# Row maxima of the masked scores: the unread output goes to the scores' own PSUM bank instead of SBUF

## The chip, the cores and the metric

One Trainium2 chip, of which the program uses one core. The metric is the device time of one execution in microseconds (us). Times of engines, tiles and waits come from a hardware profile of one execution. The engines are PE (matrix products), PEld (PE's weight loads), DVE (VectorE), ACT (ScalarE), POOL (GpSimd) and SP (which issues DMAs). PSUM is the memory that PE writes to, in banks of 512 fp32 per partition; SBUF is the other on-chip memory.

## What is computed

A transformer block on 2048 tokens of width 576: a modulated layer norm, causal attention in four segments of 512 tokens with 32 heads of width 18 and a running memory, a second layer norm, and a feed-forward part of width 4608. What matters here is the softmax inside a segment:

```python
for s in range(N):                                   # 4 segments of L = 512
    qs, ks, vs = q[:, :, s], k[:, :, s], v[:, :, s]
    logits = jnp.einsum("bhqd,bhkd->bhqk", qs, ks) * scale + mask
    p = _softmax(logits, axis=-1)
    a_dot = jnp.einsum("bhqk,bhkd->bhqd", p, vs)
    ...
    o = g * a_mem + (1.0 - g) * a_dot
```

The softmax needs the maximum of each row of masked scores.

## The kernel before

The work is cut into 32 units: four segments times eight groups of four heads. Each unit goes through two passes.

**Pass 1 (`p1_step`, lines 208 to 233)** finds the row maxima. For each of the four blocks of 128 query rows, from the last (`i = 3`, 512 keys) to the first (`i = 0`, 128 keys), PE computes scores of each head into a PSUM bank (L218; the tile is called `s` in the profile, tag `s1`, three banks in turn). DVE then makes one pass over each head's scores (L223): it adds the causal mask `tri`, takes the maximum along the row, and puts that into a column of `mx`. The instruction shows as two rows, the pass itself (CUSTOM_DVE_ANT_0) and the reading of its accumulator (DVE_READ_ACCUMULATOR2_ANT, tile `mx`). It also has to write the masked scores somewhere, and nobody reads them. With 512 and 384 keys a bank holds one head, with 256 keys two heads and with 128 keys four, so a unit has 16 DVE passes on 11 banks: four banks of 512, four of 384, two of 256 and one of 128.

After a unit's last pass POOL negates and splits the maxima (L229 to L232, tile `mc`), PE transposes them (L238, tile `pmt`), ACT copies them out (L242, `mr`) and two DMAs write them as extra rows under the unit's queries. **Pass 2 (`p2_step`)** multiplies keys by these extended queries (L715), so that the scores come out with the maximum subtracted; ACT takes the exponential (L722, tile `Pt`), POOL clears what the mask hides (L726) and PE multiplies by the values (L739, `av`).

Where the work stands:

- Units 0 and 1 do pass 1 in the first stage, beside the projections (L113). There `jp` is None, and the unread output is always the same 512 bf16 of a scratch tile (`xw`).
- Units 2 to 31 do pass 1 in the attention stage, one unit for each turn of the loop over `u` (L1509), two units ahead of pass 2. A turn has 11 steps `k`. Each step issues a bit of pass 2, then one bank of pass 1, and then the events of the table `PAT`: output projection of earlier segments (L857), memory terms (L925), weights of the output projection (L1020 to L1022), stores, and so on. So the 256-key and 128-key banks stand in steps 8 to 10, at the end of a turn. The order is written out by hand; each engine works through its own list in that order.
- In that stage the unread output goes to tiles called `junk`, bf16, four buffers in turn (`jb` is 4).

A DVE instruction that writes where an earlier DVE instruction wrote waits for that one on DVE's own semaphore. With one scratch tile the earlier one is the pass just before; with four buffers it is four passes back.

Of the kernel before, what the change touches and what calls it, by code (L numbers as in the profile page):

```python
# [9 lines left out]
BF16 = mybir.dt.bfloat16  # L10
# [5 lines left out]
P = 128  # L16
# [6 lines left out]
L = 512  # L23
# [55 lines left out]
def f32(ap):  # L79
    return ap.bitcast(F32)  # L80
# [3 lines left out]
def block(ctx: ExitStack, tc: tile.TileContext, x, wqk, wv, wo, beta, wgu, wgr, wd, c, crow, w_mod, w_mod0, w_mod1, w_modc, xt, out):  # L84
    nc = tc.nc
    def pool(stk, name, bufs=1, **kw):
        return stk.enter_context(tc.tile_pool(name=name, bufs=bufs, reuse_waits="tile", **kw))
# [42 lines left out]
    xw = pool(ctx, "xw").tile([P, 2304], F32, tag="xw", name="xw")  # L130
# [27 lines left out]
    tri = vst.tile([P, L], F32, tag="tri", name="tri")  # L158
# [49 lines left out]
    def p1_step(u, b, i, ps, jp, jb):  # L208
        if i == 3:
            mcol[u] = (mwk.tile([P, 4, 4], F32, tag="mx", name="mx"),  # L210
                       mwk.tile([P, 2, 4, 4], F32R, tag="mc", name="mc"))
        mx, mc = mcol[u]
        n = 128 * (i + 1)
        per = L // n if n <= 256 else 1
        for h0 in range(0, 4, per):
            bank = ps.tile([P, L], F32, tag="s1", name="s1", bufs=SB[-1])
            for h in range(h0, h0 + per):
                nc.tensor.matmul(bank[:, n * (h - h0):n * (h - h0) + n],  # L218
                                 lhsT=qst[b][0:108, h, 128 * i:128 * i + 128],
                                 rhs=kst[b][0:108, h // 2, 0:n], start=True, stop=True)  # L220
            for h in range(h0, h0 + per):
                junk = jp.tile([P, L], BF16, tag="junk", name="junk", bufs=jb) if jp else xw[:, 2000:2256].bitcast(BF16)
                nc.vector.tensor_tensor_reduce(junk[:, :n], bank[:, n * (h - h0):n * (h - h0) + n], tri[:, L - n:],  # L223
                                               1.0, -3e38, op0=ALU.add, op1=ALU.max, accum_out=mx[:, h, i:i + 1])
            if h0 + per < 4:
                yield
        if i == 0:
            eng = nc.gpsimd
            eng.tensor_scalar(mc[:, 0], mx, -1.0, 0.0, op0=ALU.mult, op1=ALU.add)  # L229
            lo = mwk.tile([P, 4, 4], F32, tag="ml", name="ml")  # L230
            eng.tensor_tensor(lo, mx, f32(mc[:, 0]), op=ALU.add)
            eng.tensor_scalar(mc[:, 1], lo, -1.0, 0.0, op0=ALU.mult, op1=ALU.add)  # L232
        yield
# [11 lines left out]
    def p1_unit(u, b, ps, tag, bufs, jp, jb):  # L245
        for i in range(4):
            yield from p1_step(u, b, 3 - i, ps, jp, jb)
        for i in range(3):
            yield
        mt_a(u, ps, tag, bufs)  # L250
        mt_b(u)
# [30 lines left out]
    with ExitStack() as p1:  # L282
# [74 lines left out]
        with ExitStack() as p0:  # L357
# [36 lines left out]
            for b in range(3):  # L394
                n = P if b < 2 else 64
# [303 lines left out]
    def p1_seq(u):  # L699
        if NE <= u < NU:  # L700
            for i in range(4):
                yield from p1_step(u, u % NB, 3 - i, ps, wk, 4)
# [798 lines left out]
    with tc.manual_schedule():  # L1501
# [69 lines left out]
        for i in range(4):  # L1571
            for h in range(2):
                for c in range(WC):
                    n = 8 * i + 4 * h + c
# [32 lines left out]
        n, nw = 0, PF  # L1607
# [216 lines left out]
```

## Time and profile before

| | |
|---|---|
| median of 3 runs | 1817.38 us (1816.68 to 1819.77) |
| the profiled execution: its time | 1818.94 us |
| its span, first to last instruction | 1816.9 us |
| PE busy | 1789.4 us (98% of the span) |
| DVE busy | 1484.1 us (82%) |
| ACT busy | 1086.4 us (60%) |
| POOL busy | 675.3 us (37%) |
| DVE passes of L223 with junk output | 480, of 484 ns on average |
| first and last of them | at 229.5 us and 550.2 us of the span |

The profiled execution took 1.56 us more than the median. Its busy times say how long instructions of an engine were under way; a matmul's end is modelled, so a busy PE is not always PE at full rate. The attention stage is the stretch from about 230 to 560 us; what comes behind it (up to 1816.9 us) is the feed-forward part, which has no instruction of the change.

### The profile page before, as it was taken

The page shows a single profiled execution, that of the slowest core. Times are in us where ns is not written, and L with a number is a line of the kernel's source. Part 1 is how long each engine was busy: PE and PEld are TensorE (multiplying, and loading weights), DVE is VectorE, ACT ScalarE, POOL GpSimd, SP SyncE. Part 2 cuts the span into 40 slices and gives each one's busy share as a digit, 9 for nine tenths or more (in the row PEclk, how much of TensorE's full clock was granted, in tenths as well). Part 3 has the DMA queues.
Part 4 walks back from the last instruction along what each step waited for, and adds up shares of the span by engine and source line. Part 5 has one row for each costly group of instructions (what it writes and reads, how often), then busy time and mean ns, then how long its engine had stood idle before and what let it go on. Part 6 is the DMA issues. An engine that isn't in the chain of part 4 may idle for free.

```text
span 1816.9 us, 31453 instructions
## 1 busy us (share of the span) xinstructions
PE 1789.4 (98%) x10627; PEld 1521.8 (84%) x10627; DVE 1484.1 (82%) x3365; ACT 1086.4 (60%) x2374; POOL 675.3 (37%) x1110
## 2 busy tenths in 40 slices
PE   7999999999999999999999999999999999999999
PEld 5888866777777888888888888888888888888888
DVE  7556388888886899889889889858888888888886
ACT  4334288878776567777777777534544544544542
POOL 3444078775467656656656656200000000000000
PEclk9999999999999999999999999999999999999999
DMA  8768766667657655455455454594334324324331
GB/s 270 258 225 281 265 209 195 195 203 227 168 167 239 209 181 171 144 175 176 142 177 174 122 168 145 168 311 148 98 105 126 98 92 130 106 80 130 107 103 53
DMA packets 146116, 306.26 MB, mean 169 GB/s; under 512 B 30917, under 2 KB 61765, under 8 KB 144165
## 3 DMA queue, kind: packets, MB, share of 16 engines
q1 hardware_dynamic: 134772, 260.19, 46.8%
q10 hardware_dynamic: 11184, 44.07, 6.2%
q8 instruction: 85, 1.39, 0.3%
q14 instruction: 75, 0.61, 0.1%
HBM read 198.69 MB, written 104.94 MB: 167 GB/s over the span
## 4 chain that ended last, share of the span: by engine, by line
PE 91%; DMA 3%; DVE 2%; ACT 1%; issue 1%; POOL 1%; SPq 0%; ACTq 0%; DVEq 0%; POOLq 0%
PE A L1343 25%; PE pd L1462 20%; PE C L1343 13%; PE B L1343 6%; PE pp L113 5%; PE s L218 4%; PE av L739 3%; PE pv L113 3%; PE s L715 3%; PE pw L857 3%; PE pd L1482 3%; DVE junk L223 1%; PE pn L925 1%; PE pm L550 1%; PE px L760 1%
## 5 line engine op out<-in xcount | busy, mean ns | idle before, releaser
L1343 PE MATMUL A<-y,wh 128*128 128x512 f32 x1152 | 404.1, 391 | 0.7 <-ACT cu L1372 0.7
L1470 DVE TENSOR_TENSOR acc<-acc,pd 128x576 f32<-128x576 f32 x327 | 245.0, 750 | 78.3 <-PE pd L1462 71.9
L1462 PE MATMUL pd<-dh,ah 128*128 128x288 f32 x896 | 267.4, 298 | 0.0
L1462 PE MATMUL pd<-dl,ah 128*128 128x288 f32 x896 | 263.7, 294 | 0.0
L1462 PE MATMUL pd<-dh,al 128*128 128x288 f32 x896 | 262.4, 293 | 0.0
L223 DVE CUSTOM_DVE_ANT_0 junk<-s,tri 128x512 bf16<-128x512 f32 (+1 forms) x480 | 207.2, 484 | 56.0 <-PE s L218 41.4
L1343 PEld LDWEIGHTS A<-y,wh 128*128 128x128 f32 x1152 | 216.2, 188 | 39.2 <-ACT cu L1372 1.1
L1304 DVE TENSOR_TENSOR wl<-O,wh 128x256 fp32r<-128x256 f32 x504 | 240.2, 480 | 1.6 <-ACT wh L1303 0.9
L1343 PE MATMUL A<-y,wl 128*128 128x512 f32 x576 | 224.5, 390 | 0.0
L722 ACT ACTIVATE Pt<-s 128x512 f32<-128x512 f32 (+1 forms) x352 | 182.6, 558 | 45.3 <-PE s L715 29.2
L1343 PE MATMUL C<-y,wh 128*128 128x512 f32 x576 | 202.7, 393 | 0.0
L1303 ACT CAST wh<-O 128x256 fp32r<-128x256 f32 x504 | 198.3, 406 | 2.0 <-POOL O L1297 1.7
L1462 PEld LDWEIGHTS pd<-dh,ah 128*128 128x128 f32 x896 | 168.1, 188 | 18.5 <-ACT pd L1438 3.9
L1462 PEld LDWEIGHTS pd<-dl,ah 128*128 128x128 f32 x896 | 169.5, 189 | 16.2
L1408 DVE TENSOR_TENSOR al<-sg,ah 128x512 fp32r<-128x512 f32 x240 | 177.2, 739 | 6.8 <-ACT ah L1407 6.5
L1297 POOL TENSOR_TENSOR O<-O 128x128 f32<-128x128 f32 x280 | 155.6, 589 | 71.1 <-DMA O<-in_wgu_dram 37.6
L1462 PEld LDWEIGHTS pd<-dh,al 128*128 128x128 f32 x896 | 169.1, 189 | 0.0
L1407 ACT CAST ah<-sg 128x512 fp32r<-128x512 f32 x240 | 149.0, 621 | 25.8 <-DVE sg L1367 24.9
L1343 PEld LDWEIGHTS C<-y,wh 128*128 128x128 f32 x576 | 108.0, 188 | 18.8
L1343 PEld LDWEIGHTS A<-y,wl 128*128 128x128 f32 x576 | 108.2, 188 | 14.9
L1343 PE MATMUL A<-y,wr 128*128 128x512 f32 x288 | 113.6, 394 | 0.0
L1343 PE MATMUL C<-y,wl 128*128 128x512 f32 x288 | 112.1, 389 | 0.0
(400 smaller groups left out, 4141.8 us busy)
## 6 DMA issues: line engine op xcount, KB each, us to landing
wr<-rD SPq DMA_DIRECT2D x216, 112.0 KB
O<-in_wgu_dram SPq DMA_DIRECT2D x36, 512.0 KB
oD<-O ACTq DMA_DIRECT2D x36, 512.0 KB
O<-oD SPq DMA_DIRECT2D x36, 512.0 KB
O<-in_wgu_dram SPq DMA_DIRECT2D x36, 384.0 KB
y<-yD SPq DMA_DIRECT2D x11, 1024.0 KB
ks<-kD SPq DMA_DIRECT2D x72, 144.0 KB
kD<-fh SPq DMA_DIRECT2D x16, 512.0 KB
```

Of the source, the lines that this page charges most:

```text
L113: nc.tensor.matmul(ps, lhsT=a, rhs=b, start=(k == 0), stop=(k == 13))
L218: nc.tensor.matmul(bank[:, n * (h - h0):n * (h - h0) + n], lhsT=qst[b][0:108, h, 128 * i:128 * i + 128], rhs=kst[b][0:108, h // 2, 0:n], s ...
L223: nc.vector.tensor_tensor_reduce(junk[:, :n], bank[:, n * (h - h0):n * (h - h0) + n], tri[:, L - n:], 1.0, -3e38, op0=ALU.add, op1=ALU.max ...
L722: nc.scalar.activation(pt[:, h:h + per, :n], bank[:, :n * per].rearrange("p (a b) -> p a b", a=per), AF.Exp, scale=SCALE)
L1297: eng.tensor_tensor(o[:, d, i, s_], o[:, a, i, s_], o[:, b, i, s_], op=op)
L1303: nc.scalar.copy(wh, o)
L1304: later.append(lambda: nc.vector.tensor_tensor(wl, o, f32(wh), op=ALU.subtract))
L1343: nc.tensor.matmul(bank, lhsT=a, rhs=b, start=(first and n == 0), stop=(n == 6), skip_group_check=not first)
L1407: nc.scalar.copy(ah, src)
L1408: later.append(lambda: nc.vector.tensor_tensor(al, src, f32(ah), op=ALU.subtract))
L1462: nc.tensor.matmul(pd[:, i, :288], lhsT=a[:, tk], rhs=w, start=(add and k == 0), stop=(k == 2), skip_group_check=not add)
L1470: nc.vector.tensor_tensor(o, o, pd[:, :, :288], op=ALU.add)
```

## The change

The row-maximum instruction writes the masked scores over the scores that it reads, in fp32, in the same part of the same PSUM bank. The tiles `junk` and the scratch output in `xw` are no longer written. The mask, the maximum and everything that reads `mx` stay.

```diff
             for h in range(h0, h0 + per):
-                junk = jp.tile([P, L], BF16, tag="junk", name="junk", bufs=jb) if jp else xw[:, 2000:2256].bitcast(BF16)
-                nc.vector.tensor_tensor_reduce(junk[:, :n], bank[:, n * (h - h0):n * (h - h0) + n], tri[:, L - n:],
+                nc.vector.tensor_tensor_reduce(bank[:, n * (h - h0):n * (h - h0) + n], bank[:, n * (h - h0):n * (h - h0) + n], tri[:, L - n:],
                                                1.0, -3e38, op0=ALU.add, op1=ALU.max, accum_out=mx[:, h, i:i + 1])
```

The order of the instructions on each engine stays the same in the attention stage; what differs is which instruction waits for which. These are rows of DVE's list at the end of a unit in that stage, before the change: the second pass of a bank of 256 keys, and the first and second of the bank of 128 keys (`_2766` and `_2790` are bank numbers; the names in brackets are the engines whose semaphores an instruction waits for).

```order
L773 TENSOR_TENSOR o_2512<-px,r_2758 128x4x72 [waits DMAHW4_49,DMAHW3_49,DMAHW7_49,DVE_49,Activation_49]
L223 ISA junk,mx<-s_2766,tri 128x256 [waits PE_49]
L223 ISA mx 128x1
L223 ISA junk,mx<-s_2766,tri 128x256
...
L223 ISA junk,mx<-s_2790,tri 128x128 [waits DVE_49,PE_49]
...
L223 ISA junk,mx<-s_2790,tri 128x128 [waits DVE_49]
```

The second 256-key pass waits for nothing, and the 128-key passes wait for the pass four places back that wrote the same buffer. The same place with the change (its lines are numbered one lower):

```order
L772 TENSOR_TENSOR o_2512<-px,r_2734 128x4x72 [waits DMAHW4_49,DMAHW3_49,DMAHW7_49,DVE_49,Activation_49]
L222 ISA s_2742,mx<-s_2742,tri 128x256 [waits PE_49]
L222 ISA mx 128x1
L222 ISA s_2742,mx<-s_2742,tri 128x256 [waits DVE_49]
...
L222 ISA s_2762,mx<-s_2762,tri 128x128 [waits PE_49]
...
L222 ISA s_2762,mx<-s_2762,tri 128x128 [waits DVE_49]
```

Two passes on one bank now both write that bank, so the later one waits for the one directly in front of it: in a unit the second pass of each 256-key bank and the last three passes of the 128-key bank. In the first stage it is the other way round: there every pass waited for the one before it (one scratch tile), and now only passes on a shared bank do. There the scheduler also moves a few instructions by one or two places.

## The prediction

> **What bounds the kernel now.** I start with the page: busy times and the chain that ended last.
>
> ```profile
> PE 1789.4 (98%) x10627; PEld 1521.8 (84%) x10627; DVE 1484.1 (82%) x3365; ACT 1086.4 (60%) x2374; POOL 675.3 (37%) x1110
> PE 91%; DMA 3%; DVE 2%; ACT 1%; issue 1%; POOL 1%; SPq 0%; ACTq 0%; DVEq 0%; POOLq 0%
> ```
>
> PE carries the end. The change touches DVE only, and only in the stretches where L223 stands, so next come the busy times by window for the attention stage (columns: length, then PE, PEld, DVE, ACT, POOL busy with instruction counts) and, for the same stage, the chain's shares by line.
>
> ```profile
> 230.00:330.00 100.00, 95.28 (x722) 66.35 (x721) 83.83 (x368) 86.02 (x192) 77.78 (x137) 1.00 0.66 200
> 330.00:430.00 100.00, 98.88 (x787) 77.32 (x787) 82.04 (x354) 79.02 (x172) 68.76 (x129) 1.00 0.66 202
> 430.00:530.00 100.00, 98.82 (x791) 76.60 (x790) 85.72 (x362) 76.72 (x164) 54.86 (x106) 1.00 0.67 190
> by line: PE s L218 18.4%; PE av L739 17.7%; PE s L715 15.8%; PE pw L857 10.4%; DVE junk L223 5.7%; PE pn L925 3.9%; PE px L760 3.3%; ACT Pt L722 3.2%; DMA xr<-in_x_dram 3.1%; issue 3.0%; DMA woraw<-in_wo_dram 1.7%; PE pv L113 1.2%; DMA rD<-
> ```
>
> PE is busy 95 to 99% there and DVE 82 to 86%. The passes of L223 are nevertheless 5.7% of the chain over these 335 us, 19 us: DVE is close behind PE, and sometimes ahead of it in the chain. Who waits for whom (total us, times, longest):
>
> ```profile
> DVE junk L223 <- PE s L218: 41.4, 26, 14.8
> PEld s L218 <- DVE mx L223: 10.7, 37, 1.0
> L223 DVE CUSTOM_DVE_ANT_0 junk<-s,tri 128x512 bf16<-128x512 f32 x120 | 77.1, 681 | 53.7 <-PE s L218 39.7 <-POOL mc L232 4.9 <-POOL yh L1161 4.3
> ```
>
> PE's weight loads wait for DVE 37 times, DVE waits for PE longer. The last row says where: the idle time of DVE lies ahead of 512-key passes, that is at the start of a unit. Without the very first wait (14.8 us) it is 38.9 us over 29 starts, **1.34 us a unit**. That gap is the cover for whatever DVE gains or loses at the end of a unit.
>
> **Part one: passes that wait for the pass in front of them.** The attention stage shows passes without such a wait, the first stage (one scratch tile) passes with it. First without, for 256 and 128 keys (columns: start, duration):
>
> ```profile
> 263.07 0.42 DVE L223 CUSTOM_DVE_ANT_0 junk<-s,tri 128x256 bf16<-128x256 f32 x1
> 263.42 0.42 DVE L223 CUSTOM_DVE_ANT_0 junk<-s,tri 128x256 bf16<-128x256 f32 x1
> ...
> 264.32 0.28 DVE L223 CUSTOM_DVE_ANT_0 junk<-s,tri 128x128 bf16<-128x128 f32 x1
> 264.53 0.29 DVE L223 CUSTOM_DVE_ANT_0 junk<-s,tri 128x128 bf16<-128x128 f32 x1
> ```
>
> And with it:
>
> ```profile
> 94.30 0.41 DVE L223 CUSTOM_DVE_ANT_0 xw<-s,tri 128x256 bf16<-128x256 f32 x1
> 94.76 0.42 DVE L223 CUSTOM_DVE_ANT_0 xw<-s,tri 128x256 bf16<-128x256 f32 x1
> ...
> 99.35 0.29 DVE L223 CUSTOM_DVE_ANT_0 xw<-s,tri 128x128 bf16<-128x128 f32 x1
> 99.68 0.29 DVE L223 CUSTOM_DVE_ANT_0 xw<-s,tri 128x128 bf16<-128x128 f32 x1
> ```
>
> Start to start is 0.35 against 0.46 us with 256 keys and 0.21 against 0.33 us with 128: the wait costs 0.11 and 0.12 us, though the durations stay. A unit gets two of the first and three of the second, 2 x 0.11 + 3 x 0.12 = **0.58 us**, and 30 units 17.4 us of DVE time. If nothing hid it the kernel would be 1% slower.
>
> [...]
>
> Most of the 0.58 us is hidden by the gap of 1.34 us. It shows where that cover is thin. These rows are starts of units (in brackets the idle time before); at 287.21 the instruction before it ends at 287.07:
>
> ```profile
> 247.70 0.69 DVE L223 CUSTOM_DVE_ANT_0 junk<-s,tri 128x512 bf16<-128x512 f32 x1 [0.37 <-PE s L218]
> 257.50 0.69 DVE L223 CUSTOM_DVE_ANT_0 junk<-s,tri 128x512 bf16<-128x512 f32 x1 [0.59 <-PE s L218]
> 286.31 0.76 DVE L1022 TENSOR_TENSOR wol<-woraw,woh 128x576 fp32r<-128x576 f32 x1 [0.39 <-ACT woh L1020]
> 287.21 0.69 DVE L223 CUSTOM_DVE_ANT_0 junk<-s,tri 128x512 bf16<-128x512 f32 x1
> 540.23 0.69 DVE L223 CUSTOM_DVE_ANT_0 junk<-s,tri 128x512 bf16<-128x512 f32 x1 [0.63 <-PE s L218]
> ```
>
> The shortfall is 0.58 - 0.37 = 0.21 at the first and 0.58 - 0.14 = 0.44 at the third, **0.65 us** together; the other two just suffice. A second way is the maxima's own path: DVE, then POOL, then PE's transpose, which stands in PE's list with everything queued behind it. Its thinnest place is the last but one unit:
>
> ```profile
> 540.28 0.20 POOL L232 TENSOR_SCALAR mc<-ml 128x16 fp32r<-128x16 f32 x1
> 540.54 0.28 PE L238 MATMUL pmt<-ident,mc 128*32 128x128 f32 x1
> ```
>
> POOL ends at 540.48, PE starts at 540.54: of 0.58 us, **0.52** reach PE. A third is the one stretch in which the chain itself runs through the end of a unit, to L1022 and the DMA whose buffer that frees (pieces of the chain: start, length):
>
> ```profile
> 262.82 0.33 DVE junk L223
> ...
> 265.04 0.68 DVE wol L1022
> 265.73 5.60 DMA woraw<-in_wo_dram
> ```
>
> All **0.58** count there. In the first stage the change takes waits away, two semaphores at a time with 512 keys, as these rows (with the wait, and without) show:
>
> ```profile
> 88.30 0.69 DVE L223 CUSTOM_DVE_ANT_0 xw<-s,tri 128x512 bf16<-128x512 f32 x1
> 89.15 0.69 DVE L223 CUSTOM_DVE_ANT_0 xw<-s,tri 128x512 bf16<-128x512 f32 x1
> ...
> 258.12 0.69 DVE L223 CUSTOM_DVE_ANT_0 junk<-s,tri 128x512 bf16<-128x512 f32 x1
> 258.73 0.69 DVE L223 CUSTOM_DVE_ANT_0 junk<-s,tri 128x512 bf16<-128x512 f32 x1
> ```
>
> That is 0.85 against 0.61, but the chain of that stage is projections on PE and meets such a pair once: **-0.24 us**. The instructions that move by a place or two there are covered by the projections; should one be late, its cost is of the same size. Sum of part one: 0.65 + 0.52 + 0.58 - 0.24 = **+1.5 us**.
>
> **Part two: a pass that writes PSUM.** No DVE instruction of before writes PSUM, so I bound it.
>
> ```profile
> L1389 ACT COPY B<-A 128x512 f32<-128x512 f32 x71 | 40.3, 568 | 45.3 <-PE A L1343 44.4
> L1372 ACT COPY tc<-A 128x512 f32<-128x512 f32 x72 | 42.2, 586 | 107.3 <-PE A L1343 107.2
> L1408 DVE TENSOR_TENSOR al<-sg,ah 128x512 fp32r<-128x512 f32 x240 | 177.2, 739 | 6.8 <-ACT ah L1407 6.5
> L469 DVE TENSOR_TENSOR hl<-x,hh 128x512 fp32r<-128x512 f32 x12 | 7.8, 686 | 13.6 <-ACT hh L468 13.6
> 68.46 1.89 DVE L469 TENSOR_TENSOR hl<-x,hh 128x512 fp32r<-128x512 f32 x3 [3.59 <-ACT hh L468]
> ```
>
> On ACT the same copy takes 568 ns into PSUM (L1389) and 586 into SBUF: -18 ns, the lower end. The most that two DVE rows of one size differ by where their data lie and who else is at work is 739 against 686: +53 ns, the upper end. The nearest row is DVE's own: three passes of L469, all in SBUF, take 1.89 us, so 0.60 from start to start, while L223, which reads PSUM, has 0.61. PSUM costs DVE 0.01 us as a source; I take **+10 ns** for it as a destination too. The chain has 19 us of such passes; their mean pitch is (0.61 + 0.48 + 0.35 + 0.21) / 4 = 0.41 (the 384-key pitch lies between its neighbours), so 46 of them: 46 x 0.01 = **+0.5 us**. The gap of 1.34 us hides the rest (16 x 0.01 = 0.16 us a unit).
>
> [...]
>
> **The sum.** 1.5 + 0.5 = +2.0 us. On the profiled execution's 1818.94 that makes 1820.9; it ran 1.56 us above the median, so in medians **1819.4 us** (+0.11%). What a measurement can tell from no change is about 0.2%, 3.6 us: below 1813.7 is faster, above 1821.0 slower.
>
> **The rivals.**
>
> *Slower: the PSUM write lengthens every pass.* At the upper end of 53 ns a unit has 16 x 0.053 = 0.85 us more, with the waits 1.43 against a gap of 1.34. DVE then sets the pace at most unit starts: 0.09 x 29 = 2.6 us if all gaps were alike; as they go from 0.14 up, I reckon twice that, 5. With 46 x 0.053 = 2.4 on the chain and 1.5 of part one that is +9: **1826.4**. It decides from about 20 ns on: 46 x 0.02 = 0.9, and the four thin starts above lose 0.3 each, 1.2, which with 1.5 makes 3.6. For it: PE waits for DVE 37 times. Against it: the ACT rows and the 10 ns. Chance 0.31.
>
> *Slower: POOL passes the delay on.* The 512-key row blames 4.9 us of unit starts on POOL mc L232, five times by the waits. If that is real, the gap there does not cover: mc itself comes later by 0.58, five times 2.9 us: +4.9, **1822.3**. Against it: these passes wait for PE too, and the last semaphore named need not be the one that held. Chance 0.10.
>
> *Slower by much: read and write take turns in the bank.* Pitches give (0.61 - 0.21) / 384 = 1.04 ns a column, 5120 columns a unit, 5.3 us more; less the gap 4 us, 30 times: near 1937. Nothing speaks for it but that no row excludes it. Chance 0.03, outside the range.
>
> *No change: the waits cost nothing.* If DVE would have stood still between two passes on one bank anyway, part one vanishes with its early gain, 0.5 us stays, **1817.8**. Against it stand the paired rows. Chance 0.04. [...]
>
> *Faster: the write to PSUM is cheap.* At ACT's -18 ns the unit loses only 0.58 - 0.29 = 0.29 us: 0.15 + 0.23 + 0.29 - 0.24 - 46 x 0.018 = -0.4, **1817.0**, still no change (0.07). To be faster by 0.2% each pass would have to lose some 80 ns, the whole fixed part of a 128-key pass (0.21 - 128 x 0.00104 = 0.08): -46 x 0.08 = -3.7. Chance 0.06, **1813.5**.
>
> **Chances and range.** Forecast 0.39, no cost 0.04, ACT's price 0.07: within 0.2% 0.50. Slower 0.31 + 0.10 + 0.03 = 0.44, faster 0.06. The range goes from 1815.8 (ACT's price and a little more) to 1828.0 (53 ns and some more shortfall).
>
> **What the profile after would show.** Part one: 256-key passes on one bank 0.46 apart, 128-key passes 0.33, and gaps at unit starts smaller by about 0.6 us; PE's waits for DVE hardly more than 10.7 us. Part two: passes of 512 keys 0.61 to 0.62 apart. Wrong if that pitch is 0.63 or more, or if waits of PE for DVE grow by several us (DVE sets the pace), or if pairs on one bank still stand 0.35 apart (no cost).

## The result, and the profile after

The changed kernel takes **1829.67 us** (median of 4 runs, 1828.49 to 1835.55) beside 1818.58 us for the kernel before on the same chip: a ratio of 1.0058, 95% interval 1.0043 to 1.0072, that is +10.5 us (the two medians lie 11.1 apart). The forecast was +2.0 us, and the time is above the top of the range. The profiled execution took 1829.53 us with a span of 1827.6. Its lines are numbered one lower: L222 is the pass, L218 still the score matmul, L237 the transpose of the maxima, L231 the last POOL step before it.

First where the loss lies. The row for the gate products of the feed-forward part, the first large work behind the attention stage, has the first and last start in it (before, then after):

```profile
L1343 PE MATMUL A<-y,wh x1152: 387/389/501, 590.1 to 1797.7; 128*128 128x512 f32 x192
```

```profile
L1342 PE MATMUL A<-y,wh x1152: 387/389/501, 600.3 to 1808.4; 128*128 128x512 f32 x192
```

The first one starts 10.2 us later and the last one 10.7: the whole loss arises ahead of 600 us. Now the page after, busy times and the chain, and the three windows of the attention stage (columns as before: PE, PEld, DVE, ACT, POOL):

```profile
PE 1794.7 (98%) x10627; PEld 1520.2 (83%) x10627; DVE 1515.2 (83%) x3365; ACT 1088.2 (60%) x2374; POOL 675.1 (37%) x1110
PE 89%; DVE 6%; DMA 2%; ACT 2%; POOL 1%; issue 1%; SPq 0%; ACTq 0%; DVEq 0%; POOLq 0%
```

```profile
230.00:330.00 100.00, 93.93 (x705) 63.23 (x705) 92.14 (x357) 83.66 (x186) 74.04 (x129) 1.00 0.66 197
330.00:430.00 100.00, 98.19 (x775) 75.38 (x777) 91.10 (x352) 78.14 (x169) 70.80 (x134) 1.00 0.64 197
430.00:530.00 100.00, 97.31 (x759) 74.46 (x751) 91.77 (x341) 74.91 (x161) 51.01 (x97) 1.00 0.63 183
```

DVE is busy 31 us more with the same 3365 instructions, its share of the chain rises from 2 to 6%, and in the stage it goes from 82 to 86% busy to 91 or 92%. PE, which had been busy 95 to 99%, loses a little in each window. What lengthened shows in the rows of the pass and of the accumulator read (min, median and max ns), of before and after:

```profile
L223 DVE DVE_READ_ACCUMULATOR2_ANT mx<- x480: 75/82/86, 230.1 to 550.4; 128x1 f32 x160
```

```profile
L222 DVE DVE_READ_ACCUMULATOR2_ANT mx<- x480: 82/141/147, 229.9 to 561.3; 128x1 f32 x160
```

The accumulator read goes from 82 to 141 ns. That is a row on which the prediction had no term at all. Its 480 x 59 ns don't simply add to DVE's busy time, since many reads run beside the next pass; what they cost shows in the distances between passes. The timeline of DVE after, at the start of a unit, at the end of the same unit and at the start of the next (start, duration):

```profile
258.31 0.70 DVE L222 CUSTOM_DVE_ANT_0 s<-s,tri 128x512 f32<-128x512 f32 x1 [0.58 <-PE s L218]
258.93 0.14 DVE L222 DVE_READ_ACCUMULATOR2_ANT mx<- 128x1 f32 x1
258.93 0.73 DVE L222 CUSTOM_DVE_ANT_0 s<-s,tri 128x512 f32<-128x512 f32 x1
259.58 0.73 DVE L222 CUSTOM_DVE_ANT_0 s<-s,tri 128x512 f32<-128x512 f32 x1
...
264.65 0.43 DVE L222 CUSTOM_DVE_ANT_0 s<-s,tri 128x256 f32<-128x256 f32 x1
265.00 0.14 DVE L222 DVE_READ_ACCUMULATOR2_ANT mx<- 128x1 f32 x1
265.00 0.47 DVE L222 CUSTOM_DVE_ANT_0 s<-s,tri 128x256 f32<-128x256 f32 x1
265.38 0.14 DVE L222 DVE_READ_ACCUMULATOR2_ANT mx<- 128x1 f32 x1
265.56 0.43 DVE L222 CUSTOM_DVE_ANT_0 s<-s,tri 128x256 f32<-128x256 f32 x1
...
266.33 0.30 DVE L222 CUSTOM_DVE_ANT_0 s<-s,tri 128x128 f32<-128x128 f32 x1
266.55 0.14 DVE L222 DVE_READ_ACCUMULATOR2_ANT mx<- 128x1 f32 x1
266.72 0.30 DVE L222 CUSTOM_DVE_ANT_0 s<-s,tri 128x128 f32<-128x128 f32 x1
...
267.33 0.75 DVE L1021 TENSOR_TENSOR wol<-woraw,woh 128x576 fp32r<-128x576 f32 x1
268.06 0.70 DVE L222 CUSTOM_DVE_ANT_0 s<-s,tri 128x512 f32<-128x512 f32 x1
```

Three things are to be seen. A **chained** pass (one that waits for no DVE instruction) starts together with the accumulator read of the pass before it. The read is now longer, and a pass that starts beside one takes 0.73 us, where the first of the unit, with no read beside it, takes 0.70. Behind such a pass the next one stands 0.65 away with 512 keys (median 0.648, before 0.611); behind the first of the unit it stands 0.62 away (258.31 to 258.93), no more than before the change (257.50 to 258.12). So the new destination costs a chained pass time almost only where a read runs beside it. A **waiting** pass starts 0.03 to 0.04 us after the read of the pass in front has ended (265.38 + 0.14 = 265.52, then 265.56; 266.55 + 0.14 = 266.69, then 266.72). So the longer read lengthens each wait in full: 128-key passes stand 0.39 apart and the second 256-key pass 0.56 behind a chained first one, where 0.33 and 0.46 were forecast. Third, at 268.06 the next unit starts without idle time: DVE goes from the last pass to L1021 and from there to the first 512-key pass. That is so at 10 of the 29 unit starts behind the first. In the kernel before it is so at none; the shortest idle time there, all counted from the last pass of a unit to the first of the next, is 0.37 us.

Last, who waits for whom in the attention stage (us, times, longest):

```profile
PEld s L218 <- DVE mx L222: 17.9, 57, 1.2
DVE s L222 <- PE s L218: 13.9, 23, 1.6
PEld pmt L237 <- POOL mc L231: 9.2, 16, 1.7
PE s L218 <- DVE mx L222: 3.5, 9, 0.9
PE pmt L237 <- POOL mc L231: 3.1, 7, 1.3
```

DVE's own idle time ahead of passes has halved: before it was 41.4 us with the first wait of 14.8, so 26.6. With the waits for POOL and the rest it was 40.2 us and is now 15.1. PE waits at two places now: for a score bank that DVE must release (17.9 + 3.5 = 21.4 us, before 10.7 + 1.7 = 12.4), and for the maxima that its transpose needs (9.2 + 3.1 = 12.3 us, before 0.3). Not every microsecond of these waits is lost, since weight loads overlap products (PEld is busy 1520.2 us and PE 1794.7 in a span of 1827.6); the waits grew by 21 us and the kernel by 10.5.

### The profile page after: what moved, and what is told of

Read it like the earlier page. It is cut to its first block, busy times and chain, and to the rows that moved or that the text cites. A ratio compares the mean times of both kernels' runs of the same rounds, so it can differ in the third digit from the quotient of the medians.

```text
span 1827.6 us, 31344 instructions
## 1 busy us (share of the span) xinstructions
PE 1794.7 (98%) x10627; PEld 1520.2 (83%) x10627; DVE 1515.2 (83%) x3365; ACT 1088.2 (60%) x2374; POOL 675.1 (37%) x1110
## 4 chain that ended last, share of the span: by engine, by line
PE 89%; DVE 6%; DMA 2%; ACT 2%; POOL 1%; issue 1%; SPq 0%; ACTq 0%; DVEq 0%; POOLq 0%
PE A L1342 25%; PE pd L1461 20%; PE C L1342 13%; PE B L1342 6%; PE pp L113 6%; DVE s L222 4%; PE pv L113 3%; PE pd L1481 3%; PE av L738 3%; PE pw L856 3%; PE s L218 3%; PE s L714 2%; ACT Pt L721 1%; PE pn L924 1%; PE pm L549 1%; DVE mx L222 1%
## 5 line engine op out<-in xcount | busy, mean ns | idle before, releaser
L222 DVE CUSTOM_DVE_ANT_0 s<-s,tri 128x256 f32<-128x256 f32 (+3 forms) x512 | 244.2, 509 | 41.0 <-PE s L218 34.2
```

Of the source, the lines that this page charges most:

```text
L222: nc.vector.tensor_tensor_reduce(bank[:, n * (h - h0):n * (h - h0) + n], bank[:, n * (h - h0):n * (h - h0) + n], tri[:, L - n:], 1.0, -3e3 ...
```

## The experiments

In the expectations the theories have letters: D is that the destination itself costs DVE time on every pass; W, that the loss comes from the waits at the end of a unit alone; M, that it reaches PE through the maxima and their transposes; B, through the score banks; F, that the width of fp32 costs it; P, that a part of any DVE time added among the wide passes (512 and 384 keys) is lost; D1 and D2, that any bank of PSUM as destination costs the time, or only the bank that is being read. "Narrow" passes have 256 and 128 keys.

The table collects what the experiments say on the question where PE waits (attention stage, weight loads and products added). The time is the ratio less 1, times the time of before on that chip.

| kernel | PE waits for banks, us | PE waits at transposes, us | time against before, us |
|---|---|---|---|
| before | 12.4 | 0.3 | |
| the change | 21.4 | 12.3 | +10.5 |
| e1: wide passes alone | 21.2 | 0.3 | +2.7 |
| e2: narrow passes alone | 12.7 | 12.5 | +6.4 |
| e3: the waits alone, in SBUF | 13.7 | 4.4 | +2.0 |
| e4: the change, transposes later | 27.0 | 1.3 | +9.1 |
| e10: e2, transposes later | 18.3 | 1.3 | +2.9 |
| e8: two-semaphore waits on wide passes, SBUF | 41.6 | 2.2 | +22.4 |

**e1_wide_psum: the change on the wide passes alone.** Narrow passes and the first stage keep their buffers.

```diff
             for h in range(h0, h0 + per):
-                junk = jp.tile(...) if jp else xw[:, 2000:2256].bitcast(BF16)
+                if jp and i >= 2:
+                    dst = bank[:, n * (h - h0):n * (h - h0) + n]
+                else:
+                    junk = jp.tile(...) if jp else xw[:, 2000:2256].bitcast(BF16)
+                    dst = junk[:, :n]
```

> In the attention stage only the passes over 512 and 384 keys (one head on a bank) write into their PSUM bank; those over 256 and 128 keys, and the first stage, write SBUF as before. So nothing new waits for the pass in front of it, and 240 passes write PSUM. Theory D (writing PSUM itself makes a DVE pass longer: 0.65 instead of 0.61 us from start to start with 512 keys, 8 x 0.037 = 0.30 us a unit): pitch 0.65 and 0.52, an accumulator read of 0.14 us behind these passes alone, and +0.5 to +3 us, since most of 0.30 us a unit is covered by the idle time of 1.34 us at a unit's start. Theory W (only the waits between passes on one bank cost something): pitch 0.61, accumulator read 0.08, no change (within 1 us of before).

Measured: 1.0015 (1.0005 to 1.0026), +2.7 us. No pass waits here that did not wait before, so this is the price of the destination alone. In the timeline the wide passes stand 0.65 apart as in the full change, and the narrow ones behind them have the short read again:

```profile
258.98 0.73 DVE L227 CUSTOM_DVE_ANT_0 s<-s,tri 128x512 f32<-128x512 f32 x1
259.63 0.14 DVE L227 DVE_READ_ACCUMULATOR2_ANT mx<- 128x1 f32 x1
259.63 0.73 DVE L227 CUSTOM_DVE_ANT_0 s<-s,tri 128x512 f32<-128x512 f32 x1
...
265.65 0.08 DVE L227 DVE_READ_ACCUMULATOR2_ANT mx<- 128x1 f32 x1
```

The extra would be 8 x 0.037 = 0.30 us a unit if every wide pass had a read beside it. By the timeline 137 of the 240 have: DVE is busy 1490.5 us here, 6.4 more than before, or 0.21 us a unit. That is far less than the gap of 1.34 us that was to hide it. Yet 0.4 of it is lost (0.1 to 0.7 by the interval), and the waits for banks grow by 9 us. D holds; the cover does not.

**e2_pairs_psum: the change on the narrow passes alone**, with the condition `if jp and i < 2`.

> The other half: in the attention stage only the passes over 256 and 128 keys write into their PSUM bank, with all the waits of the change; 512 and 384 keys and the first stage write SBUF as before. Theory D and waits together: the waiting passes stand 0.56 and 0.39 us apart, 2 x 0.21 + 3 x 0.18 = 0.96 us a unit, and +5 to +9 us of the 11. Theory W: the whole +10 to +12. If neither half comes near 11 while both together do, the loss is not the sum of the halves: each half is covered by the idle time at a unit's start, and only both use it up.

Measured: 1.0035 (1.0022 to 1.0047), +6.4 us. PE's waits (us, times, longest):

```profile
PEld s L218 <- DVE mx L227: 11.2, 40, 1.0
PEld pmt L242 <- POOL mc L236: 9.0, 15, 1.7
PE pmt L242 <- POOL mc L236: 3.5, 8, 1.3
```

The waits for banks are those of before, the waits at the transposes those of the full change. So the two halves of the change reach PE by two ways. 2.7 and 6.4, with the 0.4 of the first stage (e5), make 9.5 of the 10.5 us: nearly a sum, as far as figures can say that are each uncertain by some 2 us. W, by which this kernel would have lost nearly all, falls.

**e3_sbuf_waits: the same waits with bf16 in SBUF.** One junk buffer for each bank, so passes on one bank wait for each other as in the change.

```diff
+            junk = jp.tile(...) if jp else xw[:, 2000:2256].bitcast(BF16)
             for h in range(h0, h0 + per):
-                junk = jp.tile(...) if jp else xw[:, 2000:2256].bitcast(BF16)
```

> Nothing writes PSUM: all passes write SBUF in bf16 as before, but the passes on one bank share one of the four buffers, so that the same passes wait for the one in front of them as in the change. Theory D: 0.46 and 0.33 us from start to start as in the first stage of before, 0.58 us a unit, +1 to +3 us, as the prediction's part one had it. Theory W (the waits are the cause, where the output lies makes no difference): 0.56 and 0.39 us apart and +10 to +12 us.

Measured: 1.0011 (1.0003 to 1.0020), +2.0 us. This is part one of the prediction by itself. DVE's timeline at the end of a unit:

```profile
265.76 0.41 DVE L223 CUSTOM_DVE_ANT_0 junk<-s,tri 128x256 bf16<-128x256 f32 x1
266.11 0.08 DVE L223 DVE_READ_ACCUMULATOR2_ANT mx<- 128x1 f32 x1
266.22 0.42 DVE L223 CUSTOM_DVE_ANT_0 junk<-s,tri 128x256 bf16<-128x256 f32 x1
...
267.39 0.29 DVE L223 CUSTOM_DVE_ANT_0 junk<-s,tri 128x128 bf16<-128x128 f32 x1
267.71 0.29 DVE L223 CUSTOM_DVE_ANT_0 junk<-s,tri 128x128 bf16<-128x128 f32 x1
```

0.46 and 0.32 apart (medians 0.462 and 0.333), as the first stage of before had promised. Of 17.4 us of DVE time 2.0 are lost, 0.11 of it. The same waits with the output in PSUM (e2) lose 6.4 of about 29 us (2 x 0.18 + 3 x 0.18 for the waits, and 0.07 for two chained passes, 30 times): 0.22 of it. The added time is less than twice as long and its loss three times, though the intervals (0.03 to 0.21 of the time in e3, 0.14 to 0.3 in e2) leave room for a smaller difference. Of the 40.2 us of idle time ahead of passes 25.9 are left in e3 and 17.1 in e2.

**e4_late_transpose: the change, with the transposes one step later.** In the table of events `m` (the transpose) moves by one step of the turn; in the fourth pattern `n` (the copy behind it) and `V` (a load of queries) move with it.

```diff
-PAT = (["E", "", "m U D", "c", "n V G", ...
-       ["U E D", "f", "Q l m", "", "M0 ...
-       ["U E", "", "D m", "n V", "G c", ...
-       ["D E", "U m l n V", "G p", ...
+PAT = (["E", "", "U D", "m c", "n V G", ...
+       ["U E D", "f", "Q l", "m", "M0 ...
+       ["U E", "", "D", "m n V", "G c", ...
+       ["D E", "U l", "G p m n V", ...
```

> The changed kernel, with the transpose of a unit's maxima (event m, and n where it stands in the same step) one step later in PE's list in each of the four patterns, so that PE comes to it some 0.8 us later. Theory M (the delay reaches PE mainly by the maxima: DVE, POOL, then PE's transpose, with all of PE's list behind it): the waits of PE for POOL mc (3.1 us, 12.3 with the weight loads) go to nearly nothing and 3 to 6 us come back, about 1824 to 1827 us. Rival B (it reaches PE by the score banks that DVE gives back late): no more than 1 us comes back, 1829 to 1830 us.

Measured: 1.0050 (1.0036 to 1.0063), not to be told from the change itself. PE's waits:

```profile
PEld s L218 <- DVE mx L222: 21.7, 61, 1.2
PE s L218 <- DVE mx L222: 5.3, 11, 0.9
PEld pmt L237 <- POOL mc L231: 0.9, 2, 0.7
PE pmt L237 <- POOL mc L231: 0.4, 1, 0.4
```

The waits at the transposes went from 12.3 to 1.3 us, and those for banks from 21.4 to 27.0. The edit did what it should and the time did not follow: M falls for the change as a whole, B holds. It is the case of a wait that is removed and shows up at the next place, because the engine waited for, DVE, is as late as it was. (The profiled execution, 1833.77 us, is some 4 us above the median of this kernel, so its waits may be somewhat longer than usual.)

**e6_before_late_transpose: the same move in the kernel before**, to see that the move is free.

> The kernel before with the transposes of the maxima one step later, the same move as in the experiment on the changed kernel, which gave nothing back. If the move costs something of its own (the DMAs that carry the maxima to pass 2 start later), it shows here: +2 to +5 us, and the changed kernel's gain from it was eaten by that. If it costs nothing here (within 1 us), the delay of the changed kernel reaches PE by the score banks as soon as the transposes no longer wait, and the transposes were only the first place where it showed.

Measured: 1.0002 (0.9993 to 1.0011). It is.

**e10_pairs_late_transpose: the same move in e2**, where PE doesn't wait for banks more than before.

> The kernel in which only the passes over 256 and 128 keys write PSUM (+6.4 us), with the transposes of the maxima one step later (which cost nothing on the kernel before). There PE waits for the score banks no more than before (12.7 us with the weight loads, 12.4 before), but 12.5 us for POOL mc. Theory M (a delay at the end of a unit reaches PE by the transposes): 3 to 6 us of the 6.4 come back, 1820 to 1823.5 us. Rival B (it goes over to the next unit's first passes, where DVE's idle time is used up, and so to the banks): less than 1.5 us comes back, and PE's waits for the banks grow by 3 us or more.

Measured: 1.0016 (1.0007 to 1.0025), +2.9 us, so 3.5 of e2's 6.4 us come back. PE's waits for banks:

```profile
PEld s L218 <- DVE mx L227: 16.2, 56, 1.1
PE s L218 <- DVE mx L227: 2.1, 5, 0.7
```

The waits at the transposes went from 12.5 to 1.3 us. So with the narrow passes alone the maxima's path carries about half of the loss (the intervals are 4.0 to 8.6 us for e2 and 1.3 to 4.6 here, so the half is rough), and the other half shows at the banks (12.7 to 18.3 us).

**e5_first_stage_psum: the change in the first stage alone** (`if not jp`), for the early gain of 0.24 us.

> The change in the first stage alone (units 0 and 1, 32 passes, which write their PSUM bank in place of the one scratch tile and so wait less); the attention stage writes SBUF in four buffers as before. The prediction's part one: -0.24 us, since that stage is bound by the projections; with DVE's longer passes in PSUM about 0. Either way no change, within 1 us of before. If it were faster by 2 us or more, the waits of the first stage had cost more than the chain of before shows.

Measured: 1.0002 (0.9993 to 1.0011): nothing that can be told from zero.

**e7_fp32_sbuf: fp32 in SBUF**, two buffers in turn, to part the width from the place.

```diff
-                junk = jp.tile([P, L], BF16, tag="junk", name="junk", bufs=jb) if jp else ...
+                junk = jp.tile([P, L], F32, tag="junk", name="junk", bufs=jb) if jp else ...
...
-                yield from p1_step(u, u % NB, 3 - i, ps, wk, 4)
+                yield from p1_step(u, u % NB, 3 - i, ps, wk, 2)
```

> The unread output stays in SBUF but in fp32, with two buffers instead of four (four of fp32 don't fit); a pass then waits for the one two places back, which has long ended. Theory F (the width of the output makes the passes longer, not its place): 0.65 us from start to start with 512 keys, accumulator reads of 0.14 us, and +2 to +8 us. Theory D (the place does): 0.61 and 0.08 us as before, and no change beyond 1 us.

Measured: 1.0000 (0.9991 to 1.0008). The timeline:

```profile
257.38 0.69 DVE L223 CUSTOM_DVE_ANT_0 junk<-s,tri 128x512 f32<-128x512 f32 x1
257.99 0.08 DVE L223 DVE_READ_ACCUMULATOR2_ANT mx<- 128x1 f32 x1
257.99 0.69 DVE L223 CUSTOM_DVE_ANT_0 junk<-s,tri 128x512 f32<-128x512 f32 x1
```

0.61 apart with a read of 0.08, the rows of before. The width costs nothing and F falls; what is left is the place.

**e9_other_bank: fp32 into a PSUM bank of its own**, which no matmul uses, and one score bank fewer for pass 2 to make room.

```diff
-S1B, S2B, XB, WB = 3, 3, 2, 1
+S1B, S2B, XB, WB = 3, 2, 2, 1
...
-                junk = jp.tile(...) if jp else xw[:, 2000:2256].bitcast(BF16)
+                junk = ps.tile([P, L], F32, tag="jk", name="jk", bufs=1) if jp else xw[:, 2000:2256].bitcast(BF16)
```

> One look at the passes themselves, not at the total: in the attention stage the unread output goes in fp32 to a PSUM bank of its own, so no pass writes the bank it reads. It takes the place of one of pass 2's three score banks, and as there is one such bank every pass waits for the pass in front of it; so its total tells nothing of the change. Theory D1 (any write to PSUM lengthens a pass): accumulator reads of 0.14 us, waiting 128-key passes 0.39 us apart, as in the changed kernel. Theory D2 (reading and writing the same bank does): 0.08 us and 0.33 us, as with SBUF.

One execution took 1876.25 us, which says nothing on the change, since every pass now waits for the one before and pass 2 has lost a bank. What counts is the single instruction in DVE's timeline:

```profile
265.25 0.30 DVE L223 CUSTOM_DVE_ANT_0 jk<-s,tri 128x128 f32<-128x128 f32 x1
265.47 0.14 DVE L223 DVE_READ_ACCUMULATOR2_ANT mx<- 128x1 f32 x1
265.64 0.30 DVE L223 CUSTOM_DVE_ANT_0 jk<-s,tri 128x128 f32<-128x128 f32 x1
```

A read of 0.14 and 128-key passes 0.39 apart, the same as in the change. D1 holds: a bank that is not being read costs the same, and reading and writing the same bank adds nothing to it.

**e8_wide_waits: DVE time added among the wide passes, without PSUM.** All wide passes share one junk buffer, so that each waits for the one before it, on two semaphores.

```diff
-                junk = jp.tile([P, L], BF16, tag="junk", name="junk", bufs=jb) if jp else ...
+                if jp:
+                    junk = jp.tile([P, L], BF16, tag="junkw" if i >= 2 else "junk", name="junk", bufs=1 if i >= 2 else jb)
+                else:
+                    junk = ...
```

> All in SBUF: passes over 512 and 384 keys share one buffer and wait for the pass in front of them (two semaphores, 0.23 us more from start to start, as in the first stage of before, so up to 7 x 0.23 = 1.6 us a unit, 48 us of DVE time); those over 256 and 128 keys keep four buffers. Theory P (DVE time is covered at the end of a unit, by the idle time at the next one's start, but not among the wide passes, whose banks PE waits for): a share of 0.3 or more of the DVE time shows, +14 to +35 us, against 0.11 for the waits among the narrow passes (17 us of DVE time, +2.0 us). Rival C (only the amount against the cover of 1.34 us a unit matters): 1.6 - 1.34 = 0.3 us a unit, +8 us, no more than 12.

Measured: 1.0123 (1.0109 to 1.0137), +22.4 us. DVE's timeline near a unit's start, and then the waits:

```profile
264.03 0.69 DVE L226 CUSTOM_DVE_ANT_0 junk<-s,tri 128x512 bf16<-128x512 f32 x1
264.65 0.08 DVE L226 DVE_READ_ACCUMULATOR2_ANT mx<- 128x1 f32 x1
264.87 0.69 DVE L226 CUSTOM_DVE_ANT_0 junk<-s,tri 128x512 bf16<-128x512 f32 x1
```

```profile
PEld s L218 <- DVE mx L226: 34.5, 89, 1.7
DVE junk L226 <- PE s L218: 29.9, 21, 3.1
PE s L218 <- DVE mx L226: 7.1, 21, 1.4
```

Passes that do wait stand 0.84 apart instead of 0.61 with 512 keys (+0.23, and as much with 384). In the timeline 145 wide passes stand right behind another one and pay it, 33 us of DVE time. Two thirds of it, 22 us, are lost, while DVE's idle time ahead of passes hardly shrinks (34.5 us with 4.6 for POOL, before 40.2). That settles the question of the cover: the gap at the start of a unit hides little of what is added among wide passes. They stand one bank after the other on three banks, PE waits inside the unit for the next one, and the unit becomes longer with its gap still in it. P holds, and the rival by which only the amount counts falls: 33 us are 1.1 us a unit, less than the mean gap.

## Why the prediction was wrong, step by step

- **The failed step is part two: a PSUM destination for +10 ns a pass.** That number was a source's, 0.61 against 0.60 us for reading PSUM or SBUF, carried over to writing. Measured is +37 ns on each chained pass that has a read beside it (e1), inside the bounds of -18 and +53, and above the 20 ns from which the slow rival was to decide. e7 and e9 show that it is the place, PSUM in the bank that is read or in another, and neither the width nor the shared bank.
- **In the same step a second price was put at nothing.** The accumulator read became 59 ns longer. Waiting passes start 0.03 to 0.04 us after it has ended, so the wait grew from the forecast 0.11 and 0.12 to 0.18 (0.21 behind a pass that was itself chained to a long read). The prediction summed waits and destination as if they did not touch: 0.58 + 0.16 = 0.74 us a unit. They come to 2 x 0.21 + 3 x 0.18 + 0.21 (e1) = 1.17 us, 35 us in 30 units.
- **The slow rival was right that the destination decides, and its size is partly luck.** It reckoned 1.43 us a unit and +9 us; 1.17 us and +10.5 were measured. By the rival DVE would use up the gap and set the pace at most unit starts. It did so at 10 of 29, and at as many in e2. Compared one by one with the idle times at the 29 starts before, the 0.97 us of e2 exceed them by 2.5 us in all (an estimate from the trace of before); that is about what is left in e10 (+2.9), where the transposes are out of the way. Its sum had the transposes at one place alone and the wide passes only where they lay on the chain of before.
- **The cover was misread.** "That gap is the cover for whatever DVE gains or loses at the end of a unit" is right in the main for the narrow passes: of the 40.2 us of idle time ahead of passes 25.9 are left in e3, 17.1 in e2 and 15.1 in the change, and e3's waits lose 0.11 of their time. It is not a cover for the wide passes, though the prediction wrote that "the gap of 1.34 us hides the rest" of their time too: 38.4 us of idle time are left in e1 and 34.5 in e8, and 0.4 and two thirds of their added time are lost. And for longer narrow passes it is not enough (0.22 lost in e2): the gaps are uneven (0.37 to 2.84 us at the 29 starts in the trace of before), and PE's waits at the transposes grow from 0.3 to 12.5 us.
- **Part one held as a size**: the waits alone cost 2.0 us (0.5 to 3.6) where 0.65 + 0.52 + 0.58 = 1.75 had been worked out. Its places held less well. At the third thin start the row shown has another 0.39 us of idle time ahead of L1022, so that 0.05 and not 0.44 us should have been missing there; and PE's waits at the transposes grew from 0.3 to 4.4 us in eleven waits, not at the last but one unit alone. That the sum came out is therefore partly luck.
- **The waits cost what the paired rows of before had shown.** In e3, which differs from before in nothing but such waits, a waiting pass stands 0.12 us further behind.
- **The early gain of 0.24 us** in the first stage is too small to be seen (e5). The other rivals fell by their own signs: no pitch grew by the 1.04 ns a column that taking turns would cost, no PSUM write was cheaper, pairs on one bank did not stay 0.35 apart, and DVE's waits put down to POOL mc, 4.9 us before, did not grow but fell to 2.3 in e3 and are gone in the change.
- **What stays open.** How the loss of the full change divides between transposes and banks is not settled, since e4 shows that the one wait turns into the other. Why the accumulator read, whose own output lies in SBUF in all kernels, takes 59 ns longer is not shown. Nor is it shown why a pass with such a read beside it stands 37 ns further off.

No version ran faster than the kernel before: e5, e6 and e7 are equal to it within 0.11%, all others slower.

## What to carry to other kernels

An output that nobody reads still has a destination, and here its move from SBUF to PSUM cost 59 ns on each accumulator read and 37 ns on a chained pass beside one. Before moving it, find a row in which the same engine writes there, and if there is none, carry the whole bracket, not the price of reading from there. Add up the costs of one chain before comparing them with a gap, since a longer instruction also lengthens the wait of whoever waits for its end (0.11 and 0.12 us became 0.18 here), and compare them with each gap and not with the mean. And ask in front of which instruction a gap lies: idle time at the start of a unit hid most of what the waits at the end of the unit before added (0.11 of it was lost in e3), and much less of what was added to the passes that free banks inside the unit (0.4 lost in e1, two thirds in e8).

## What the runs showed of the hardware

- A DVE pass with an accumulator output that writes fp32 to PSUM has an accumulator read of 140 ns instead of 82, with the bank that is read as destination (e1) as with another (e9). In a chain such passes stand 37 ns further apart than with output in SBUF (0.648 against 0.611 us with 512 keys, 0.515 against 0.478 with 384), the same for both sizes; behind a pass that starts alone, with no read beside it, the distance is 0.62 us with 512 keys in both kernels.
- In SBUF, fp32 output costs what bf16 output does (e7: 0.61 us with 512 keys).
- Chained passes overlap: with 512 keys in SBUF they stand 0.61 us apart and last 0.68 to 0.69, with 256 keys 0.35 apart and 0.42. With a wait for the pass in front they don't: 256-key passes of e3 last 0.41 to 0.42 and stand 0.46 apart. The wait adds 0.11 to 0.12 us on one semaphore with the output in SBUF, 0.18 to 0.21 with it in PSUM (e2 and the change), 0.23 on two semaphores in SBUF (e8, 512 and 384 keys).
